# The 49-product in-projection for one more chunk: which chunk, which engine and which stage make its weight forms

## The chip, the cores and the metric

The kernel runs on one core of one Trainium2 chip. A core has five engines that run side by side: TensorE (PE, matmuls into PSUM), VectorE (DVE), ScalarE (ACT), GpSimd (POOL) and SyncE (SP, which issues DMAs). The metric is the device time of one execution in microseconds (us), lower is better; several executions are run and the median is given.

## The reference

Attention in which a query sees only the keys that fall to the same centroid, then a feed-forward block with the gate `h * erf(softplus(h))`. Batch 4, 8 heads, 768 positions, head size 64, all float32:

```python
q_assign = np.argmax(np.einsum('bhsd,hcd->bhsc', q_n, c_n), axis=-1)
k_assign = np.argmax(np.einsum('bhsd,hcd->bhsc', k_n, c_n), axis=-1)
mask = q_assign[:, :, :, None] == k_assign[:, :, None, :]
scores = np.where(mask, scale * np.matmul(q, k.transpose(0, 1, 3, 2)), -1000000000.0)
attn = softmax(scores)
x = np.matmul(attn, v).transpose(0, 2, 1, 3).reshape(3072, 512)
h = x @ w_in                                   # 512 -> 2048
sp = np.maximum(h, 0.0) + np.log1p(np.exp(-np.abs(h)))
out = (h * erf(sp)) @ w_out                    # 2048 -> 512
```

(`softmax` stands for the shifted exponentials and their division.) The change lies in the second part, `x @ w_in`, and in the work around it.

## The kernel before

**Attention** takes the first 408 us: 16 periods, one for each pair of heads of a batch. The transposed result x goes to a DRAM buffer, `x_dram`. Beside it the weights are converted and laid down in SBUF, and sums and differences of blocks of `w_in` ("left forms") are made, on DVE and on POOL. Ten conversion steps of `w_out` are left for later.

**The feed-forward part** takes the 3072 tokens in 6 chunks of 512. Each chunk has an in-projection (x times `w_in`), the gate (curves on ACT, products on DVE) and an out-projection. Products of 2x2 blocks are done with seven multiplications in place of eight (Strassen's scheme in Winograd's form), for which blocks are first added and subtracted; these sums are called *forms*. There are three ways of doing it:

- `hidden(n, lot)` does half an in-projection: 4 column groups of 7 products each, 28 products of two 128x128x256 matmuls. Each product goes to one of 8 PSUM banks in turn (`bank()`, six named `bank` and two named `turned`) and is then added into the output tile `g` by DVE or copied by ACT. `project(n, lot, pace)` does half an out-projection in the same way. While products are issued, other work is put between them, one item or more behind each product, from a list written by hand (`aside_work`).
- `hidden26` is `hidden` for chunks 1 and 2, and `project26` is an out-projection of 26 products, for chunks 1 to 5. Its right-hand forms are made once, on POOL, and streamed from DRAM (`b_dram`) through three SBUF places (`ring`).
- `hidden49(n)` does a whole in-projection with two levels of the scheme: 49 slots (`SLOTS`), each four 128x128x128 matmuls. It needs forms of the forms of `w_in`. With an outer form `o` (seven of them, the left forms of `w_in`), the inner ones are b12 - b11 (5), b22 - that (6), that - b21 (4) and b22 - b12 (7). Forms 4, 5 and 6 of each `o` lie in DRAM (`w_dram`, 21 blocks of 256 KB) and are streamed through `ring` (`load_twice`); form 7 takes the place of b12 in SBUF.

`TWICE = 3`: chunks 3, 4 and 5 use `hidden49`. Their forms are made by `forms_twice` on POOL: four of the 28 behind chunk 1's in-projection, the other 24 during chunk 2's, in a free x tile with four places; SP stores each to `w_dram`. `last_form_twice` then copies the seven forms 7 back from DRAM into `w_in`, when chunk 2's in-projection has read it for the last time.

**What orders the work.** Each engine runs its instructions in program order (`InOrder` wraps PE, DVE, ACT, POOL and one handle of SP, `sy`); DMAs issued by `nc.sync` itself may be put elsewhere in SP's queue. What matters around the change:

- The ten late conversion steps of `w_out`: each is a fetch by SP into one of four places, `size` and `rest` and `sign` on ACT, `bounded` and `shifted` on DVE, and `summed` on POOL, behind which the fetch of the step four later is issued. `weights(n)` lists them, `all_weights(lo, hi)` joins them.
- `out_forms[f]`: four POOL operations each, forms of `w_out`. `out_forms[0]` and `[1]` run in chunk 0's first in-projection half, `[2]` and `[3]` in chunk 1's first, behind a one-column POOL operation (`fence`) that waits for this half's first result.
- x tiles: `x_of[n]` are two buffers (`x_own`). `load_x(n)` reads a chunk's x from `x_dram`; `right_forms` of it are four operations.
- `a_s` (one buffer) holds the gate's curves.

All instructions carry line 132, that of the helper that records them, so the profile is read by the names of tiles. The order of stages is written out at the end of the kernel: chunk 0's in-projection halves, its first out-projection half, chunk 1's first in-projection half, chunk 0's second out-projection half, and then the loop over chunks.

Of the kernel before, what the change touches and what calls it, by code (L numbers as in the profile page):

```python
# [19 lines left out]
P = 128  # L20
# [94 lines left out]
WHERE = {"x": (0, 0), "u": (0, 1), "w": (1, 1)}  # L115
TWICE = 3
AHEAD = 4
BY_VECTOR = 4
GROUPS = (((1, 2), (1, 5, 6, 3, 7, 2, 4)), ((6, 7, 4), (1, 2, 5, 6, 3, 7, 4)), ((3, 5), (1, 5, 6, 3, 7, 2, 4)))
SLOTS = [(i, o) for inner, outer in GROUPS for o in outer for i in inner]  # L120
# [20 lines left out]
def kernel(  # L141
# [634 lines left out]
    def idle(n):  # L776
        return [lambda: None] * n
# [39 lines left out]

    ring, extra = [], []
    x_extra, spare_more = {}, []
    w_dram = dram.tile([len(STREAMED) + len(STEPS), P, FG * P], F32, name="w_dram")  # L820
    b_dram = dram.tile([N_STREAM + len(KEPT), P, FG * HM], F32, name="b_dram")
# [93 lines left out]

    def hidden26(n, lot, generation=(), later=()):
        generation = list(generation)
# [18 lines left out]
        else:  # L936
            aside_work.extend(paired([]))
        def begin():
            if later:
                fence(n)  # L940
            for work in later:
                work()

        hidden(n, lot, {0: begin, 1: middle})
        finish_aside()
# [23 lines left out]

    def forms_twice():  # L970
        t = xp.tile([P, DM // P, CT], F32, name="x_own").rearrange("p k t -> p (k t)")
        places = [t[:, i * FG * P : (i + 1) * FG * P] for i in range(4)]

        def made(o, i):
            w = lefts(*w_in_parts(0, HF))[o]
            b11, b12, b21, b22 = (w[:, k, f * FG * P : (f + 1) * FG * P] for k in range(2) for f in range(2))
            t, a, b = {
                5: (places[0], b12, b11), 6: (places[1], b22, places[0]),
                4: (places[2], places[1], b21), 7: (places[3], b22, b12),
            }[i]  # L980
            minus_of(t, a, b, ge)
            k = STREAMED.index((i, o)) if i < 7 else len(STREAMED) + STEPS.index(o)
            nc.sync.dma_start(out=w_dram[k], in_=t)

        return [functools.partial(made, o, i) for o in STEPS for i in (5, 6, 4, 7)]

    def last_form_twice():
        for o in STEPS:
            w = lefts(*w_in_parts(0, HF))[o]
            nc.sync.dma_start(out=w[:, 0, FG * P :], in_=w_dram[len(STREAMED) + STEPS.index(o)])  # L990

# [82 lines left out]
    def hidden49(n):  # L1074
# [3 lines left out]
        free = [banks[(k + i) % len(banks)] for i in range(len(banks))]  # L1078
        x_extra[n] = xp.tile([P, DM // P, CT], F32, name="x_own")
        x_forms, x_form = x_twice(n)  # L1080
# [125 lines left out]
    def project26(n):  # L1206
# [15 lines left out]
        else:  # L1222
            curves, products_at = gate_after(n)
        if n + 1 >= TWICE:
            load_x(n + 1)
        between = []
        if n + 1 < NCHUNK:
            parts = x_parts(n + 1)
            between = right_forms(ve, *parts)
            if n + 1 >= TWICE:  # L1230
                between = negated_last(between, ve, parts[2], parts[4])
        tiles = [(N_STREAM * (n - 1) + j + 2) % RING for j in range(N_STREAM)]
        banks26 = {}
# [35 lines left out]
        for p, r in enumerate(RIGHT):  # L1269
# [26 lines left out]
            if p >= len(RIGHT) - 4 and between:  # L1296
                between.pop(0)()
            if p == 12 and n + 2 < TWICE:
                load_x(n + 2)
        for p in sorted(banks26):  # L1300
# [188 lines left out]
    fetch(PLACES - 1)  # L1489
    queues[0] = queues[1] = nc.sync  # L1490
    for p in range(NPAIR):
        for i in range(HJ * 2):
            period(p, i)
        if p == LAST_X:
            load_x(0)
            load_x(1)
        if p == LAST_X + 2:
            forms += zip(*(right_forms(e, *x_parts(0)) for e in (ve, ge)))
# [28 lines left out]
    def weights(n):  # L1527
        return [
            functools.partial(w, N_EARLY + n) for w in (size_and_rest, bounded, sign, shifted, summed)
        ]  # L1530

    def all_weights(lo, hi):
# [3 lines left out]

    def fence(n=1):
        t = up.tile([P, HM], F32, name="u")
        g = g_of[n, 0, 0][:, 0, 0, 0:1]
        ge.tensor_tensor(out=t[:, 0:1], in0=g, in1=g, op=ALU.add)  # L1540
# [13 lines left out]
    finish_aside()  # L1554
    aside_work += gates(0, 0, (1,), right_forms(ve, *x_parts(1))) + gates(0, 1, (0,))
    project(0, 0, 3)
    finish_aside()
    aside_work += together(gates(0, 1, (1,)), idle(2) + [fence] + out_forms[2] + out_forms[3])
    take_places(2)
# [15 lines left out]
    for n in range(1, NCHUNK):  # L1575
        if n >= TWICE:
            hidden49(n)
        else:
            if n > 1:
                hidden26(n, 0, (), making if n + 1 == TWICE else ())  # L1580
            hidden26(n, 1, making if n == 1 else ())
        if n + 1 == TWICE:
            last_form_twice()
        if n + 2 == TWICE:
            making = forms_twice()
            for work in making[:AHEAD]:
                work()
            del making[:AHEAD]
        project26(n)
# [32 lines left out]
```

## Time and profile before

| | |
|---|---|
| median of 3 runs | 964.53 us (964.52 to 964.92) |
| profiled execution | 964.84 us, of which the profiled span is 963.1 us |
| TensorE | busy 954.6 us of the span |
| VectorE | busy 792.3 us |
| ScalarE | busy 535.9 us |
| GpSimd | busy 520.2 us |
| bytes read from and written to HBM | 86.54 MB and 26.21 MB |

TensorE's stages, by the start of the first matmul of each:

| starts at (us) | stage | length (us) |
|---|---|---|
| 407.95 | chunk 0 in-projection, two halves | 49.23 |
| 457.18 | chunk 0 out-projection, first half | 24.27 |
| 481.45 | chunk 1 in-projection, first half | 24.18 |
| 505.63 | chunk 0 out-projection, second half | 24.17 |
| 529.80 | chunk 1 in-projection, second half | 24.38 |
| 554.18 | chunk 1 out-projection | 44.95 |
| 599.13 | chunk 2 in-projection (`hidden26`, two halves) | 48.35 |
| 647.48 | chunk 2 out-projection | 44.89 |
| 692.37 | chunk 3 in-projection (`hidden49`) | 43.77 |
| 736.14 | chunk 3 out-projection | 45.19 |
| 781.33 | chunk 4 in-projection (`hidden49`) | 43.77 |

How to read the profile's rows: a row of an engine's instructions in order of time has the start (us from the start of the span), the duration (us) of the instruction or of a run of like ones, engine, line, operation, `out<-in` by the names of tiles with their shapes, the count, and in brackets the engine's idle time before it and what ended that. A float32 matmul shows as two records. PE's durations include the drain of its pipeline, so the distance between starts is the pace. In a row of windows each engine has its busy time and, in brackets, its instructions.

POOL by stage before: it is busy to 441.7 us nearly without a break, then works on single `summed` operations until 461.3, is idle to 484.2, busy from there to 560.5, idle to 601.6, busy to 634.

### The profile page before, as it was taken

What the parts mean: (1) busy time and instruction counts of PE and PEld (TensorE: products, weight loads), DVE (VectorE), ACT (ScalarE), POOL (GpSimd) and SP (SyncE); (2) the same over time, 40 slices, a digit from 0 to 9 for tenths busy, and PEclk for the clock granted to TensorE, in tenths of its full rate; (3) what the DMA queues carried; (4) which work ended last, traced back from release to release, by engine and by line L of the source; (5) the groups of instructions that cost most, each with busy time, mean ns of one, the idle gap of its engine ahead of it and who ended that gap; (6) DMA issues with size and microseconds to landing.
All of it is one profiled execution on the core that took longest, in us unless ns stands there. A gap on an engine that the chain in (4) does not pass through costs nothing.

```text
span 963.1 us, 22126 instructions
## 1 busy us (share of the span) xinstructions
PE 954.6 (99%) x8786; PEld 726.6 (75%) x8786; DVE 792.3 (82%) x1407; ACT 535.9 (56%) x806; POOL 520.2 (54%) x360
## 2 busy tenths in 40 slices
PE   8999999999999999999999999999999999999998
PEld 3555555555555555588888888888999899989987
DVE  8888888888888886879879888668868987896887
ACT  3777777777777665557614432354257236625541
POOL 1688888887788888845189920930054015202600
PEclk9999999999999999999999999999999999999999
DMA  9455444444444311051103454553445346344533
GB/s 211 87 111 111 111 111 110 108 109 106 89 111 111 67 35 35 19 182 45 44 1 153 154 197 138 222 198 104 160 123 173 110 132 208 110 144 122 159 113 110
DMA packets 171303, 114.20 MB, mean 119 GB/s; under 512 B 131264, under 2 KB 140992, under 8 KB 171200
## 3 DMA queue, kind: packets, MB, share of 16 engines
q1 hardware_dynamic: 168704, 112.36, 41.2%
q8 instruction: 69, 1.13, 0.5%
q10 hardware_dynamic: 2496, 0.43, 0.2%
q14 instruction: 34, 0.28, 0.1%
HBM read 86.54 MB, written 26.21 MB: 117 GB/s over the span
## 4 chain that ended last, share of the span: by engine, by line
PE 97%; DVE 1%; DMA 1%; SPq 0%; issue 0%; ACT 0%; DVEq 0%
PE bank L132 43%; PE turned L132 31%; PE sc L132 17%; PE wide L132 6%; DVE nmx L132 1%; DMA in_k<-in_k_dram 0%; SPq L132 0%; DMA in_q<-in_q_dram 0%; DVE kT L132 0%; DVE sims L132 0%; DVE qT L132 0%; DVE km L132 0%; DVE turned L132 0%; DVE wide L132 0%; ACT qm L132 0%
## 5 line engine op out<-in xcount | busy, mean ns | idle before, releaser
L132 POOL TENSOR_TENSOR more_out<-more_out,pr 128x768 f32<-128x768 f32 x128 | 217.3, 1697 | 18.5 <-ACT pr L132 9.9
L132 DVE TENSOR_REDUCE nmx<-wide 128x2 f32<-128x768 f32 x189 | 180.5, 955 | 47.9 <-PE wide L132 47.0
L132 ACT ACTIVATE pr<-sc 128x768 f32<-128x768 f32 x192 | 148.7, 810 | 94.0 <-PE wide L132 77.1
L132 PE MATMUL turned<-pr,in_v 128*32 128x193 f32 x3072 | 144.8, 330 | 0.0
L132 POOL TENSOR_TENSOR g<-g 128x512 f32<-128x512 f32 x27 | 35.4, 1310 | 178.8 <-DVE g L132 177.4
L132 PEld LDWEIGHTS turned<-pr,in_v 128*32 128x32 f32 x3072 | 91.5, 109 | 50.8 <-issue 21.3
L132 PE MATMUL sc<-qT,kT 64*128 64x384 f32 x528 | 98.3, 486 | 0.0
L132 DVE TENSOR_TENSOR g<-g 128x512 f32<-128x512 f32 x114 | 79.1, 694 | 19.8 <-PE bank L132 16.3
L132 DVE TENSOR_TENSOR g<-bank,g 128x256 f32<-128x256 f32 (+1 forms) x146 | 67.2, 476 | 27.3 <-PE bank L132 12.2
L132 PE MATMUL bank<-x_own,w_in 128*128 128x128 f32 (+1 forms) x464 | 83.8, 322 | 0.0
L132 DVE TENSOR_TENSOR g<-a_s,g 128x512 f32<-128x512 f32 x84 | 77.0, 938 | 3.6 <-ACT a_s L132 3.6
L132 PE MATMUL bank<-g_more,g 128*128 128x256 f32 x336 | 79.4, 379 | 0.0
L132 POOL TENSOR_TENSOR more_out<-pr,pr 128x768 f32<-128x768 f32 x32 | 60.4, 1886 | 28.1 <-ACT pr L132 28.1
L132 PEld LDWEIGHTS bank<-x_own,w_in 128*128 128x128 f32 x464 | 70.0, 191 | 6.0 <-issue 0.6
L132 PEld LDWEIGHTS bank<-g_more,g 128*128 128x128 f32 x336 | 63.8, 190 | 8.7
L132 ACT ACT_TABLE_LOAD x42 | 53.9, 1283 | 29.6 <-DVE g L132 29.0
L132 PE MATMUL bank<-w_out,g 128*128 128x256 f32 x296 | 69.3, 380 | 0.0
L132 ACT ACTIVATE a_s<-g 128x1024 f32<-128x1024 f32 (+1 forms) x38 | 42.7, 1143 | 45.5 <-POOL g L132 34.7
L132 PEld LDWEIGHTS <-qv 64*128 64x128 bf16 x384 | 27.0, 93 | 52.9 <-issue 36.7
L132 PEld LDWEIGHTS sc<-qT,kT 64*128 64x128 f32 x528 | 49.9, 187 | 21.4 <-ACT inv L132 2.4
L132 PE MATMUL wide<-kv,qv 64*128 64x384 bf16 x378 | 64.1, 328 | 1.3 <-DVE nmx L132 0.6
L132 PE MATMUL wide<-km,qm 64*128 64x384 bf16 (+1 forms) x378 | 62.6, 327 | 0.0
(236 smaller groups left out, 2004.9 us busy)
## 6 DMA issues: line engine op xcount, KB each, us to landing
g_more<-b_dram SPq DMA_DIRECT2D x48, 512.0 KB, 3.3
g_more<-w_dram SPq DMA_DIRECT2D x63, 256.0 KB, 2.9
w_dram<-x_own SPq DMA_DIRECT2D x28, 256.0 KB, 2.0
x_own<-in_moe_w_in_dram SPq DMA_DIRECT2D x13, 512.0 KB, 4.4
in_v<-in_v_dram SPq DMA_DIRECT2D x32, 192.0 KB, 3.1
x_dram<-more_out SPq DMA_DIRECT2D x128, 48.0 KB, 1.9
x_own<-x_dram SPq DMA_DIRECT2D x6, 1024.0 KB, 5.4
in_k<-in_k_dram SPq DMA_DIRECT2D x59, 96.0 KB, 2.8
```

The source lines that it names most:

```text
L132: ins = getattr(self.engine, name)(*args, **kw)
```

## The change

`TWICE` becomes 2: chunk 2 takes `hidden49` too, so only chunk 1 keeps the 28-product halves.

- The streamed forms 4, 5 and 6 of six of the seven outer forms (18 in all) are now made on POOL in chunk 0's in-projection: four right behind the attention (stored by `sy`), and 3, 3, 1, 1, 0, 1, 3, 2 of them ahead of the first eight `summed` (`MADE_BEFORE`, stored by `nc.sync`). Their places are the free `a_s` tile (four) and chunk 1's x tile `x_of[1]` (four, used again in turn).
- The three of the last outer form are made on POOL in chunk 1's out-projection, behind products 0, 2 and 4, and stored through ACT's queue two products later (`REST_AT`, `STORE_AFTER`).
- Form 7 is made in place by DVE, seven operations in chunk 1's out-projection behind products 3, 6, ..., 21 (`LAST_AT`); it no longer passes through DRAM, and `w_dram` has 21 blocks in place of 28.
- Since `x_of[1]` is used as a staging place, chunk 1's x is loaded behind chunk 0's in-projection, no longer in the attention, and its `right_forms` run in the second half of chunk 0's first out-projection instead of the first.
- `out_forms[2]` runs behind chunk 0's in-projection, ahead of that load.
- During the attention SP's loads keep their program order (`sy`).

```diff
-TWICE = 3
-AHEAD = 4
+TWICE = 2
+MADE_BEFORE = (3, 3, 1, 1, 0, 1, 3, 2, 0, 0)
+LAST_AT = (3, 6, 9, 12, 15, 18, 21)
+EARLY_OUTERS = 6
+STORE_AFTER = 2
+REST_AT = (0, 2, 4, 6, 8, 10, 12, 14, 16, 18, 20, 22)
...
-    def forms_twice():
-        t = xp.tile([P, DM // P, CT], F32, name="x_own").rearrange("p k t -> p (k t)")
-        places = [t[:, i * FG * P : (i + 1) * FG * P] for i in range(4)]
...
-        return [functools.partial(made, o, i) for o in STEPS for i in (5, 6, 4, 7)]
-
-    def last_form_twice():
-        for o in STEPS:
-            w = lefts(*w_in_parts(0, HF))[o]
-            nc.sync.dma_start(out=w[:, 0, FG * P :], in_=w_dram[len(STREAMED) + STEPS.index(o)])
+    def forms_twice(outers, staged):
+        places = [t[:, i * FG * P : (i + 1) * FG * P] for t in staged for i in range(4)]
+        n = 0
+        for o in outers:
+            w = lefts(*w_in_parts(0, HF))[o]
+            b11, b12, b21, b22 = (w[:, k, f * FG * P : (f + 1) * FG * P] for k in range(2) for f in range(2))
+            new = [places[n + i if n + i < len(places) else -4 + (n + i) % 4] for i in range(3)]
+            n += 3
+            for i, t, a, b in zip((5, 6, 4), new, (b12, b22, new[1]), (b11, new[0], b21)):
+                minus_of(t, a, b, ge)
+                yield functools.partial(store_queue[0].dma_start, out=w_dram[STREAMED.index((i, o))], in_=t)
+
+    def last_forms_twice():
+        work = {}
+        for o, p in zip(GROUPS[1][1], LAST_AT):
+            w = lefts(*w_in_parts(0, HF))[o]
+            b12, b22 = (w[:, k, FG * P :] for k in range(2))
+            work.setdefault(p, []).append(functools.partial(minus_of, b12, b22, b12, ve))
+        return work
...
+        making = {}
+        if n + 1 == TWICE:
+            x_extra[TWICE] = xp.tile([P, DM // P, CT], F32, name="x_own")
+            making = last_forms_twice()
+            store_queue[0] = ae
+            forms = forms_twice(GROUPS[1][1][EARLY_OUTERS:], [x_extra[TWICE].rearrange("p k t -> p (k t)")])
...
+            for p in REST_AT[: 3 * (len(STEPS) - EARLY_OUTERS)]:
+                making.setdefault(p, []).append(form)
+                making.setdefault(p + STORE_AFTER, []).append(store)
...
-            if p == 12 and n + 2 < TWICE:
-                load_x(n + 2)
+            for work in making.get(p, ()):
+                work()
...
-    queues[0] = queues[1] = nc.sync
+    queues[0] = queues[1] = sy
...
         if p == LAST_X:
             load_x(0)
-            load_x(1)
...
-            functools.partial(w, N_EARLY + n) for w in (size_and_rest, bounded, sign, shifted, summed)
+            functools.partial(w, N_EARLY + n) for w in (size_and_rest, bounded, sign, shifted, summed_after_forms)
         ]
+
+    making = forms_twice(
+        GROUPS[1][1][:EARLY_OUTERS],
+        (actp.tile([P, 2 * FG * HT], F32, name="a_s"), x_of[1].rearrange("p k t -> p (k t)")),
+    )
+    for _ in range(4):
+        next(making)()
+    queues[0] = store_queue[0] = nc.sync
+
+    def summed_after_forms(n):
+        for _ in range(MADE_BEFORE[n - N_EARLY]):
+            next(making, idle(1)[0])()
+        summed(n)
...
     finish_aside()
-    aside_work += gates(0, 0, (1,), right_forms(ve, *x_parts(1))) + gates(0, 1, (0,))
+    for store in making:
+        store()
+    for work in out_forms[2]:
+        work()
+    load_x(1)
+    aside_work += gates(0, 0, (1,)) + gates(0, 1, (0,), right_forms(ve, *x_parts(1)))
     project(0, 0, 3)
     finish_aside()
-    aside_work += together(gates(0, 1, (1,)), idle(2) + [fence] + out_forms[2] + out_forms[3])
+    aside_work += together(gates(0, 1, (1,)), idle(2) + [fence] + out_forms[3])
...
-            if n > 1:
-                hidden26(n, 0, (), making if n + 1 == TWICE else ())
-            hidden26(n, 1, making if n == 1 else ())
-        if n + 1 == TWICE:
-            last_form_twice()
-        if n + 2 == TWICE:
-            making = forms_twice()
-            for work in making[:AHEAD]:
-                work()
-            del making[:AHEAD]
+            hidden26(n, 1, making)
         project26(n)
```

## The prediction

> **What bounds the kernel now.** I read the page's busy times and its chain of waits first, then each engine's instructions in order of time from 400 us on. The page says that TensorE (PE) is the bound:
>
> ```profile
> span 963.1 us, 22126 instructions
> PE 954.6 (99%) x8786; PEld 726.6 (75%) x8786; DVE 792.3 (82%) x1407; ACT 535.9 (56%) x806; POOL 520.2 (54%) x360
> ...
> PE 97%; DVE 1%; DMA 1%; SPq 0%; issue 0%; ACT 0%; DVEq 0%
> ```
>
> 97% of the chain that ended last is matmul, so a saved matmul is saved time, and any other engine costs time only where it makes PE wait. The gain is read from the starts of PE's stages. These rows begin chunk 2's in-projection (old form), chunk 2's out-projection, chunk 3's in-projection (49 products), its out-projection, and chunk 4's in-projection:
>
> ```profile
> 599.13 1.03 PE L132 MATMUL turned<-x_own,w_in 128*128 128x256 f32 x4
> 647.48 1.89 PE L132 MATMUL turned<-more_out,g_more 128*128 128x256 f32 x8
> 692.37 1.95 PE L132 MATMUL bank<-x_own,w_in 128*128 128x128 f32 x16
> 736.14 1.89 PE L132 MATMUL bank<-more_out,g_more 128*128 128x256 f32 x8
> 781.33 1.84 PE L132 MATMUL bank<-x_own,w_in 128*128 128x128 f32 x15
> ```
>
> The old in-projection takes 647.48 - 599.13 = 48.35 us (56 products of 0.864), the new one 736.14 - 692.37 = 43.77 us (49 slots of 0.893).
>
> The other view is the end of chunk 0's second in-projection half, where PE has no slack left:
>
> ```profile
> 450.15 1.03 PE L132 MATMUL bank<-x_more,w_in 128*128 128x256 f32 x4
> 456.20 1.03 PE L132 MATMUL bank<-x_more,w_in 128*128 128x256 f32 x4
> 457.18 1.13 PE L132 MATMUL bank<-w_out,g 128*128 128x256 f32 x4
> ...
> 456.72 0.41 DVE L132 TENSOR_TENSOR g<-g,bank 128x256 f32<-128x256 f32 x1
> 445.00:457.00 12.00, 12.00 (x57) 10.43 (x55) 12.00 (x25) 6.94 (x9) 2.59 (x2) 1.00 0.13 44
> ```
>
> Products rotate over 8 PSUM banks. The product begun at 450.15 is the 21st of this half, and the first product of the out-projection, 8 later, reuses its bank. It starts at 457.18 and not at 456.20 + 0.864 = 457.06: it waits for DVE's eviction, which ends at 456.72 + 0.41 = 457.13. The windows row (columns PE, PEld, DVE, ACT, POOL) has DVE busy 12.00 of 12.00 us there. So DVE is one whole bank rotation behind, and **any delay of DVE before 456.72 is PE's delay in full**. Nothing wins it back, since PE is the chain afterwards.
>
> What can delay DVE there is POOL:
>
> ```profile
> 449.10 1.31 POOL L132 TENSOR_TENSOR w_out<-w_out,osb 128x512 int32<-128x512 int32 x1 [4.48 <-DVE w_out L132]
> 455.23 1.28 POOL L132 TENSOR_TENSOR w_out<-w_out,osb 128x512 int32<-128x512 int32 x1 [4.82 <-DVE w_out L132]
> 437.74 1.46 POOL L132 TENSOR_TENSOR w_out<-w_out 128x512 f32<-128x512 f32 x1
> 553.73 1.71 POOL L132 TENSOR_TENSOR x_own<-w_in 128x512 f32<-128x512 f32 x1
> ...
> 449.22 1.74 DVE L132 TENSOR_TENSOR g_more<-g 128x512 f32<-128x512 f32 x1
> 451.22 0.68 DVE L132 TENSOR_TENSOR g_more<-g_more,g 128x512 f32<-128x512 f32 x1
> ```
>
> A DVE addition on 128x512 with both inputs in SBUF takes 0.68 us while POOL idles (451.22). Begun just after POOL's (449.22 after 449.10), it ends 0.55 us after POOL's end. TENSOR_SCALAR does likewise: 0.41 us alone, else POOL's end + 0.28 (435.15 took 1.49). Operations that read PSUM stay at 0.41 beside a busy POOL. POOL pays as well: its pitch of 1.24 us (432.63, 433.86, 435.09) grows by 0.18 for a TENSOR_SCALAR let in (437.74) and by 0.45 for an addition (553.73 to 558.76, and pairs of 3.41 where quiet pairs take 2.50). One such DVE operation gets in per POOL operation. The Trainium skill (SBUF — State Buffer, "Who interferes with whom") calls this an exclusive lock on a port pair shared by VectorE and GpSimd: a VectorE instruction with two SBUF inputs, or in a two-port mode, fully blocks behind a GpSimd instruction. The rows agree, and this rule speaks against the change; without it the sum would be the bare -4.3 us.
>
> **The change part by part.** *Chunk 2's in-projection*: -(48.35 - 43.77) = -4.58 us. Its DVE, ACT, POOL and stream loads (20 more) are those of chunks 3 to 5, whose 49 slots ran without a gap on PE.
>
> *The out-projection behind it* lasts 647.48 to 692.37 = 44.89 now; the two that follow 49 products and precede others last 736.14 to 781.33 and 825.10 to 870.29, 45.19 each. +0.30 us.
>
> *Removed at no price*: 28 POOL forms and stores at 553.7 to 634, and 7 copies back through DRAM at 642 to 647. PE waited for none.
>
> *18 forms on POOL in chunk 0*: 4 behind the last attention sums (which end at 403.05 + 8.39 = 411.44), then 3, 3, 1, 1, 0, 1, 3, 2 ahead of summed 0 to 7. POOL's order up to the 18th form is 18 forms, 7 sums and 8 out-forms = 33 operations. A triple of forms takes 605.70 - 601.78 = 3.92 (one reads the result just made: pitch 1.35), so 6 x 3.92 = 23.5; 7 sums x 1.24 = 8.7; 8 out-forms, 2 of them at 1.35, 10.1. Together 42.3. In this time DVE wants in with 15 TENSOR_SCALARs (bounded and shifted 0 to 6, bounded 7) and 8 additions (an x form, four gate products, three left forms): 15 x 0.18 + 8 x 0.45 = 6.3. POOL ends at 411.44 + 48.6 = 460.0, without a pause, where it now idles 4.48 and 4.82 us.
>
> From 444 us on DVE then gets one SBUF operation per POOL operation, and its seventh bounded ends at 460.0 + 0.28. To the 21st eviction it has left (starts 0.33 apart, 0.60 for an addition): an eviction 0.33, an addition 0.60, two evictions 0.66, shifted 0.33, an eviction 0.33, bounded 8 behind POOL's next sum 1.2, the eviction 0.33 = 3.8. That is 464.1 against 457.13: +7.0. If the let-in operations fill the 12 gaps of 0.11 behind dependent forms (1.3), +5.7. I take +6.4, the middle. High end: the ninth form waits for the fifth's place to be stored; if that store stands in SP's queue behind the x_dram writes of 420.52, all comes 1 us later, +8.0. Low end: 33 x 1.24 = 40.9 with nothing paid for what is let in; POOL ends at 452.4, the eviction at 456.5, below today's, so 0.
>
> Earlier, in the first half, I find no PE wait: there the eviction most behind ends 3.2 us after its product (417.32 against 414.1), my delays add up to 1.9 by 424, and the limit is 7 x 0.864 = 6.05. By 433.5 DVE has caught up.
>
> *The sums behind the forms, and their fetches*: summed 4 slides from 440.40 to about 446, and the fetch behind it by 4 us; ACT's read of that place at 446.94 slips 3 us, but the DVE work that waits for it stands at 455.35 now and about 461 then. Nothing.
>
> *Chunk 1's x load and forms* move past SP's queue behind the forms' stores: the last store about 462, the load of 5.4 us (page, 1024 KB) lands at 468; DVE comes to these four additions at 471.5 + 6.4. They fall where DVE idled 2.94 us (before 475.74). If the load came 10 us later, DVE and so PE would stand behind it.
>
> *Four out-forms* (5.1 us) go from POOL at 484 to about 467, ahead of the gate products at 466.11, which ACT moves on with PE. At most 0.3 us late, where the first product that needs all four comes 1.7 us later. Nothing.
>
> *Chunk 1's out-projection*: seven in-place subtractions on DVE, 7 x 0.60 = 4.2 us, against 6.1 us of DVE idle there (1.98 before 563.02, 0.68, 0.36, 0.18, 1.63 before 588.97, 0.73, 0.58). Three forms on POOL instead of four. Three stores issued by ACT, each 4 us after its form by position, and ACT is busy 11.13 of 24.7 us in 559.0 to 583.7: evictions queue behind them, none late. Nothing; bounds 0 and what rival C gives.
>
> *SP's queue in attention* takes its loads in written order and the x load at 306.38 is gone. in_v is issued at 340.58 and the next at 364.92, each a period of 24.3 us ahead of use. Nothing; bound in rival D.
>
> **The sum**, against the profiled execution's own 964.84 us (span 963.1, 1.7 around it): 964.84 - 4.58 + 0.30 + 6.4 = 966.96. That execution lay 0.31 above the median of the runs, 964.53, so I say **966.7**. 0.2% of the time, 1.93 us, is about what a measurement of this kernel can tell from no change.
>
> **The rivals.** *A, the forecast*: the wait moves to PE at 452 to 464 us. With a delay of 4 to 8.3 us it gives 964.2 to 968.6; chance 0.66.
>
> *B, the other side*: DVE keeps its place, because POOL's pauses absorb the forms. For it: POOL is idle 9.3 us between 444.6 and 455.2. Against: 33 operations fill them. It decides from a delay under 2.3 us: 964.53 - 4.28 + 0 to 2.3 = 960.2 to 962.6; 0.25.
>
> *C, slower by chunk 1's out-projection*: the seven DVE subtractions wait as 449.22 does, 7 x 1.42 = 9.9 against 6.1 of idle, and carry 3.8 us into the 49 products. Banks there come free about 5 us ahead (evicted at 699.8, reused at 704.9), so it decides only with 1.2 us more, say behind ACT's stores. On top of A up to 3 us, 968 to 970; 0.05.
>
> *D, no gain arrives*: chunk 2's streamed forms, or a load in attention, come late. Against: 99% PE in chunks 3 to 5 and in attention. A plus 1 to 4.6; 0.04.
>
> **How the numbers follow.** A lies 0.41 above 966.46, 0.24 within, 0.01 below. B gives 0.23 faster and 0.02 same; C and D 0.07 slower, 0.02 same. Faster 0.24, same 0.28, slower 0.48. The range 961.8 to 968.6 leaves out the lower half of B (0.12) and C and D's upper part (0.07); A's own is 964.2 to 968.6.
>
> **What would show it.** Right: POOL without a pause from 411 to about 460; additions of DVE at 1.3 to 1.5 us there; PE gaps between 452 and 464 of some 6 us in all, and the first `bank<-w_out,g` of chunk 0 near 463.5; chunk 2's in-projection 43.8 us; nothing else on PE. Wrong: that first product still near 457 (then B), or PE gaps near 600 (C) or before 400 (D). In those gaps the Trainium skill (TensorE: Matmul & The Clock Gate, "What's actually happening") would halve the clock after an idle window of some 3.4 us; my longest gap is about 2.2 us, and the page's clock row is 9 throughout, so I add nothing for it.

## The result, and the profile after

The changed kernel takes **967.92 us** (median of 7 runs, 967.59 to 968.93); the kernel before, timed beside it, 964.89 us (7 runs). The ratio is 1.0035, 95% interval 1.0023 to 1.0046: slower by 0.35%. The prediction was 966.7 us. The profiled execution after takes 967.78 us, of which the span is 966.1 us, 3.0 more than before.

The same parts of the page as before, for the changed kernel (busy times by engine, then the chain of waits):

```profile
span 966.1 us, 22439 instructions
PE 953.0 (99%) x8954; PEld 729.1 (75%) x8954; DVE 810.8 (84%) x1399; ACT 540.8 (56%) x815; POOL 536.7 (56%) x370
...
PE 93%; DVE 3%; DMA 1%; ACT 1%; issue 1%; SPq 0%; DVEq 0%; ACTq 0%
```

PE is busy 1.6 us less (953.0 for 954.6), yet the span is longer: the saved matmuls are there, and so are new waits. In the chain PE's share falls from 97 to 93%, and DVE's rises from 1 to 3%. Where the waits stand is read from the starts of PE's stages, in the profiled executions:

| stage | before | after | difference |
|---|---|---|---|
| up to chunk 0's in-projection | 407.95 | 407.41 | -0.54 |
| chunk 0's in-projection | 49.23 | 56.54 | **+7.31** |
| chunk 0's and 1's next four halves | 97.00 | 96.80 | -0.20 |
| chunk 1's out-projection | 44.95 | 44.90 | -0.05 |
| chunk 2's in-projection | 48.35 | 43.77 | **-4.58** |
| chunk 2's out-projection | 44.89 | 45.19 | +0.30 |
| chunk 3's in-projection | 43.77 | 44.35 | +0.58 |
| all behind it | 226.96 | 227.14 | +0.18 |

The gain is exactly there. These are PE's instructions in order of time at the borders of chunk 2's in-projection, its first product and the first of its out-projection: 649.42 - 605.65 = 43.77 us.

```profile
605.65 0.61 PE L136 MATMUL turned<-x_own,w_in 128*128 128x128 f32 x4
649.42 1.89 PE L136 MATMUL turned<-more_out,g_more 128*128 128x256 f32 x8
```

The loss is at the end of chunk 0's in-projection. First PE, at the stage's start and there, with its idle time and what ended it in brackets, then POOL and DVE in the same stretch: 463.95 - 407.41 = 56.54 us.

```profile
407.41 1.99 PE L136 MATMUL bank<-x_own,w_in 128*128 128x256 f32 x8
...
453.27 1.13 PE L136 MATMUL bank<-x_own,w_in 128*128 128x256 f32 x4 [1.77 <-DVE g L136]
454.96 1.13 PE L136 MATMUL bank<-x_more,more_in 128*128 128x256 f32 x4 [0.56 <-DVE g L136]
456.65 1.13 PE L136 MATMUL bank<-x_own,w_in 128*128 128x256 f32 x4 [0.56 <-DVE g L136]
459.73 2.07 PE L136 MATMUL turned<-x_more,more_in 128*128 128x256 f32 x4 [1.95 <-DVE g L136]
461.60 1.66 PE L136 MATMUL turned<-x_own,more_in 128*128 128x256 f32 x4
463.09 1.03 PE L136 MATMUL bank<-x_more,w_in 128*128 128x256 f32 x4
463.95 2.32 PE L136 MATMUL bank<-w_out,g 128*128 128x256 f32 x10
...
457.47 1.59 POOL L136 TENSOR_TENSOR x_own<-x_own,w_in 128x512 f32<-128x512 f32 x1
461.41 1.28 POOL L136 TENSOR_TENSOR w_out<-w_out,osb 128x512 int32<-128x512 int32 x1 [2.35 <-DVE w_out L136]
...
453.14 1.43 DVE L136 TENSOR_TENSOR g_more<-g 128x512 f32<-128x512 f32 x1
456.52 1.42 DVE L136 TENSOR_TENSOR g<-g 128x512 f32<-128x512 f32 x1
459.60 0.67 DVE L136 TENSOR_TENSOR g_more<-g,g_more 128x512 f32<-128x512 f32 x1
462.90 0.41 DVE L136 TENSOR_TENSOR g<-g,bank 128x256 f32<-128x256 f32 x1
```

And the row of windows that had POOL busy 2.59 of 12 us before:

```profile
445.00:457.00 12.00, 9.11 (x41) 7.06 (x40) 12.00 (x15) 7.85 (x10) 11.92 (x8) 1.00 0.48 175
```

PE waits four times for DVE, for 4.84 us in all; the first of these waits ends at 453.27. DVE is busy without a break in either kernel, but does 15 instructions in these 12 us where it did 25: its additions with both inputs in SBUF take 1.42 to 1.44 us while POOL (now 11.92 us busy) makes forms, and 0.67 us at 459.60, half a microsecond after POOL's last form has ended (457.47 + 1.59 = 459.06). The eviction at 462.90, the one that releases the bank of the first out-projection product, ends 463.31, which is 55.90 us after the in-projection's start; before it was 457.13, or 49.18 after. So DVE is 6.72 us late.

Where this time goes can be added up. From DVE's last short pause (443.61 before, 443.70 after) to that eviction it does the same 26 operations in both kernels; the times are from each start to the next, in us:

| DVE's operations | before | after |
|---|---|---|
| 13 that read a PSUM bank | 4.34 | 4.31 |
| 8 additions and products with both inputs in SBUF | 6.39 | 9.26 |
| 5 TENSOR_SCALARs on `w_out` | 2.71 | 5.93 |
| together | 13.44 | 19.50 |

So 6.06 of the 6.72 us are longer SBUF operations of DVE in this stretch, and operations on PSUM take what they took. The other 0.6 us it brings along: its last pause of any size is 1.73 us for ACT before 440.88 (0.88 before 440.43 in the kernel before), and ACT had itself waited for DVE's `g` before its curve at 434.02. Neither of these waits ended with a transfer, and after 443.7 DVE does not wait at all.

PE is 7.31 late, 0.6 more. The rest is the clock. A row of windows per microsecond (the column behind the engines is the granted clock, the first of the last three):

```profile
459.00:460.00 1.00, 0.27 (x1) 0.27 (x2) 1.00 (x3) 0.00 (x0) 0.06 (x1) 0.72 0.08 31
460.00:461.00 1.00, 1.00 (x3) 0.82 (x4) 1.00 (x4) 0.00 (x0) 0.00 (x0) 0.50 0.59 231
461.00:462.00 1.00, 1.00 (x3) 0.76 (x3) 1.00 (x3) 0.00 (x0) 0.59 (x1) 0.50 0.00 0
462.00:463.00 1.00, 1.00 (x4) 0.80 (x3) 1.00 (x2) 0.00 (x0) 0.69 (x1) 0.57 0.75 61
```

From 459.45 to 462.86, by the trace's record of the clock, it is at half. The products begun at 459.73 and 461.60 take 1.87 and 1.49 us from start to start in place of 0.864. The last products before the out-projection then end late by themselves, and its first one starts 0.64 us after the eviction, where before it was 0.05.

### The profile page after: what moved, and what is told of

Its sections match the earlier page's. It is cut to its first block, busy times and chain, and to the rows that moved or that the text cites. A ratio compares the mean times of both kernels' runs of the same rounds, so it can differ in the third digit from the quotient of the medians.

```text
span 966.1 us, 22439 instructions
## 1 busy us (share of the span) xinstructions
PE 953.0 (99%) x8954; PEld 729.1 (75%) x8954; DVE 810.8 (84%) x1399; ACT 540.8 (56%) x815; POOL 536.7 (56%) x370
## 4 chain that ended last, share of the span: by engine, by line
PE 93%; DVE 3%; DMA 1%; ACT 1%; issue 1%; SPq 0%; DVEq 0%; ACTq 0%
PE bank L136 40%; PE turned L136 31%; PE sc L136 17%; PE wide L136 6%; DVE g L136 1%; DVE w_out L136 1%; DVE nmx L136 1%; DMA out_dram<-osb 0%; ACT a_s L136 0%; DMA in_k<-in_k_dram 0%; DVE osb L136 0%; SPq L136 0%; DMA in_q<-in_q_dram 0%; DVE kT L136 0%; ACT g_more L136 0%
## 5 line engine op out<-in xcount | busy, mean ns | idle before, releaser
L136 POOL TENSOR_TENSOR g<-g 128x512 f32<-128x512 f32 x36 | 47.1, 1309 | 217.5 <-DVE g L136 215.6
L136 PE MATMUL bank<-w_out,g 128*128 128x256 f32 x328 | 75.7, 380 | 0.0
L136 DVE TENSOR_TENSOR g<-bank,g 128x256 f32<-128x256 f32 (+1 forms) x129 | 63.7, 522 | 13.1 <-PE bank L136 5.9
L136 PE MATMUL bank<-x_own,w_in 128*128 128x128 f32 (+1 forms) x432 | 72.0, 309 | 2.3 <-DVE g L136 2.3
L136 PE MATMUL bank<-g_more,g 128*128 128x256 f32 x304 | 71.8, 379 | 0.0
L136 PEld LDWEIGHTS bank<-w_out,g 128*128 128x128 f32 x328 | 62.1, 190 | 9.6 <-issue 1.4
L136 PEld LDWEIGHTS bank<-x_own,w_in 128*128 128x128 f32 x432 | 60.9, 192 | 7.0 <-DVE g L136 3.1
L136 PEld LDWEIGHTS bank<-g_more,g 128*128 128x128 f32 x304 | 57.8, 190 | 7.8
```

What stands on the lines that cost most here:

```text
L136: ins = getattr(self.engine, name)(*args, **kw)
```

## The experiments

All medians and ratios are against the kernel before, run on the same chip beside it. "Early" forms are POOL's weight forms in chunk 0's in-projection; the changed kernel has 18 of them there and 3 in chunk 1's out-projection.

**1. Are POOL's forms the cause, or the DMAs that go with them?** The 18 subtractions are left out, and 18 stores copy a block of `w_in` in their place, so what chunks 2 to 5 compute is not the reference's result.

```diff
-                minus_of(t, a, b, ge)
+                if len(staged) == 1:
+                    minus_of(t, a, b, ge)
+                else:
+                    t = b11
                 yield functools.partial(store_queue[0].dma_start, out=w_dram[STREAMED.index((i, o))], in_=t)
```

> The 18 early subtractions on POOL are left out (chunks 2 to 5 read streamed forms that are only copies of a block of w_in), but all 18 stores, their places in SP's queue, the later load of chunk 1's x and the seven in-place subtractions of DVE stay. Port theory (DVE waits behind POOL's instructions): POOL is as free as before the change in 411 to 461 us, the first out-projection product of chunk 0 comes 49.2 to 49.6 us after the start of the in-projection, as before (49.23; with the change 56.54), and the time is 964.9 - 4.3 + 0 to 0.7 = 960.6 to 961.3. Rival, DMA theory (256 KB stores delay the fetches of the late weight steps, ACT reads them late, and that is what DVE and PE wait for): the 56.5 us and about 968 stay.

Measured: 960.38 us, ratio 0.9955 (0.994 to 0.9969). The in-projection takes 49.11 us, the other stages are as after within 0.3 us. The first products of this stage and of the next, and then the stores (duration, then first and last start):

```profile
407.87 1.99 PE L136 MATMUL bank<-x_own,w_in 128*128 128x256 f32 x8
456.98 3.19 PE L136 MATMUL bank<-w_out,g 128*128 128x256 f32 x14
...
L1559 SPq DMA_DIRECT2D w_dram<-more_in x9: 337/432/457, 344.2 to 369.4; - x9
L1559 SPq DMA_DIRECT2D w_dram<-w_in x5: 319/394/637, 74.1 to 371.0; - x5
L136 SPq DMA_DIRECT2D w_dram<-w_in x4: 439/536/917, 413.2 to 414.9; - x4
```

The edit took out more than it was meant to. A store of a block of `w_in` waits for no form, so 14 of the 18 left the stage with the forms: they are issued in the attention, by 371 us, and four at 413. The run shows that the whole +7.3 goes with the forms and their stores together, and that the later x load and the shifted out-forms cost nothing. Between forms and stores it does not decide; experiment 2 and DVE's times above do. It also gives the full worth of the 49 products: about -4.4 us.

**2. Is it what POOL reads, or that POOL is busy?** Each of the 18 subtractions becomes two memsets, which write the same place and read nothing; the streamed forms are then constants.

```diff
-                minus_of(t, a, b, ge)
+                if len(staged) == 1:
+                    minus_of(t, a, b, ge)
+                else:
+                    for _ in range(2):
+                        ge.memset(t, 0.5)
```

> Each of the 18 early subtractions on POOL is replaced by two writes of a constant into the same place (so the streamed forms of chunks 2 to 5 are constants): POOL is busy in the same places and reads nothing. If only POOL's reads hold up DVE's additions, as the port rule has it, the DVE additions of 444 to 460 us that fall beside a write last 0.7 us and not 1.4, TENSOR_SCALARs may still wait, and the first half of the delay goes: 51 to 54 us from the in-projection's start to the first out-projection product. If POOL's order alone (the sums behind the forms, the fetches behind the sums) sets the delay, it depends on POOL's time only: with writes as long as the subtractions (2 x 0.6 us) 56 us. If any POOL instruction blocks DVE, 55 to 57 us.

Measured: 961.92 us, 0.997 (0.9959 to 0.9981); in-projection 51.72 us in the profiled execution (962.9 us, the slowest of eight). Here all 18 stores are issued in the stage, from 413.2 to 456.6 us, as in the changed kernel, so they and what they push back cost 2.6 of the 7.4 us at the most. POOL, then DVE, in order of time:

```profile
449.44 3.48 POOL L136 MEMSET x_own<- 128x512 f32 x6
452.88 1.30 POOL L136 TENSOR_TENSOR w_out<-w_out,osb 128x512 int32<-128x512 int32 x1
...
449.97 0.85 DVE L136 TENSOR_SCALAR w_out<-w_out 128x512 uint32<-128x512 uint32 x1
451.07 0.68 DVE L136 TENSOR_TENSOR g_more<-g 128x512 f32<-128x512 f32 x1
452.00 0.68 DVE L136 TENSOR_TENSOR g_more<-g_more,g 128x512 f32<-128x512 f32 x1
452.94 1.79 DVE L136 TENSOR_TENSOR g<-g 128x512 f32<-128x512 f32 x1
```

Beside memsets an addition with two inputs in SBUF takes its 0.68 us; beside the next POOL operation that reads two (452.88) it takes 1.79. TENSOR_SCALAR (0.41 alone) waits even for a memset. In the stretch added up above, the 26 operations take 16.80 us (19.50 after, 13.44 before): the additions and products 7.34, near the 6.39 of before, the TENSOR_SCALARs 5.13, near the 5.93 of after. So most of the loss, not all of it, goes with POOL's reads, and what is left stands in DVE's operations again. The shares are not exact, since POOL is also done earlier, at 456.55 us in place of 459.06. The Trainium skill (SBUF — State Buffer, "Who interferes with whom") states both halves of this: a VectorE instruction with two SBUF inputs contends with a GpSimd instruction that reads SBUF and not with one that only writes it, while tensor_scalar in a two-port mode needs the shared pair itself. The four durations above agree with it.

**3. Fewer early forms.** Twelve early, nine in chunk 1's out-projection.

```diff
-MADE_BEFORE = (3, 3, 1, 1, 0, 1, 3, 2, 0, 0)
-EARLY_OUTERS = 6
+MADE_BEFORE = (3, 3, 1, 1, 0, 0, 0, 0, 0, 0)
+EARLY_OUTERS = 4
```

> Only 12 forms early (4, then 3, 3, 1, 1 ahead of the first four sums; none in the second in-projection half), the other 9 in chunk 1's out-projection. Port theory: out-forms still end at about 444.4 us, then POOL has only the sums; DVE meets two more busy POOL instructions than before the change: the in-projection lasts 49.2 + 1 to 2 us, and the time is 964.9 - 4.3 + 1 to 2 + 0 to 0.7 = 961.6 to 963.3, if nine forms on POOL in chunk 1's out-projection cost nothing (its 44.9 us stay). Rival: POOL's forms cost the same wherever they lie; then chunk 1's out-projection grows by 3 us or more and the time stays at 967 to 968.

Measured: 964.65 us, 1.0 (0.999 to 1.0009), outside what was expected. The in-projection takes 51.27 us as expected, but chunk 1's out-projection takes 47.66 in place of 44.90. PE in that stage:

```profile
572.45 1.99 PE L136 MATMUL turned<-g_more,g 128*128 128x256 f32 x8 [0.72 <-DVE g L136]
582.90 3.69 PE L136 MATMUL bank<-w_out,g 128*128 128x256 f32 x16 [1.54 <-DVE g L136]
```

**4. The forms where POOL and DVE both have room.** Nine early, in POOL's pauses; six right behind the in-projection, where DVE idles 3 us waiting for ACT's curves; six in chunk 1's out-projection. `out_forms[2]` goes back to its old place.

```diff
-MADE_BEFORE = (3, 3, 1, 1, 0, 1, 3, 2, 0, 0)
-EARLY_OUTERS = 6
+MADE_BEFORE = (1, 2, 1, 1, 0, 0, 0, 0, 0, 0)
+EARLY_OUTERS = 5
+FIRST_OUTERS = 3
...
-    for work in out_forms[2]:
-        work()
     load_x(1)
-    aside_work += gates(0, 0, (1,)) + gates(0, 1, (0,), right_forms(ve, *x_parts(1)))
+    middle = forms_twice(
+        GROUPS[1][1][FIRST_OUTERS:EARLY_OUTERS], (x_of[0].rearrange("p k t -> p (k t)"),)
+    )
+
+    def made():
+        next(middle)()
+
+    aside_work += gates(0, 0, (1,)) + together(
+        gates(0, 1, (0,), right_forms(ve, *x_parts(1))), [made] * (3 * (EARLY_OUTERS - FIRST_OUTERS))
+    )
     project(0, 0, 3)
     finish_aside()
-    aside_work += together(gates(0, 1, (1,)), idle(2) + [fence] + out_forms[3])
+    aside_work += together(gates(0, 1, (1,)), idle(2) + [fence] + out_forms[2] + out_forms[3])
```

> Nine forms early, laid into POOL's pauses (4, then 1, 2, 1, 1), six in chunk 0's first out-projection half, where POOL idled from 461 to 484 us, through the x tile that chunk 0 no longer needs, and six in chunk 1's out-projection; the second group of out-forms goes back to where it was. Port theory: POOL's out-forms end about 1.3 us later than before the change, the in-projection lasts 49.2 + 0 to 1 us; in the out-projection half a bank is reused after 8 x 1.73 us, so six blocked DVE additions (6 x 0.8 = 5 us) do not reach PE. Time 964.9 - 4.3 + 0 to 1 + 0 to 0.7 = 960.6 to 962.3, faster than both kernels. Rival: the wait only moves into the out-projection half, which grows by 2 to 5 us: 963 to 967.

Measured: 962.65 us, 0.998 (0.997 to 0.9989): faster than both kernels, and 0.35 us above the expected 960.6 to 962.3. The in-projection takes 49.11 us, the same as with no form at all, and the half behind it 24.22. What is left is in chunk 1's out-projection, 49.08 us in the profiled execution (the slowest of the ten). There PE waits once:

```profile
571.20 3.25 PE L137 MATMUL turned<-g_more,g 128*128 128x256 f32 x8 [2.13 <-DVE g L137]
```

Behind that wait the clock (0.50) falls in this execution, as the window of the next microsecond shows; the other nine have a mean clock of 0.999 or 1.000 where this one has 0.998.

```profile
572.00:573.00 1.00, 1.00 (x4) 0.74 (x4) 0.97 (x2) 0.00 (x0) 0.00 (x0) 0.50 0.00 0
```

**5. The last six held back** until product 12 of that stage, by a one-column POOL operation that reads an output tile.

In 4's kernel:

```diff
-REST_AT = (0, 2, 4, 6, 8, ...)
+REST_AT = (12, 13, 14, 15, 16, 17)
...
+            def hold():
+                t = up.tile([P, HM], F32, name="u")
+                o = osb_of[n, 0][:, 0, 0:1]
+                ge.tensor_tensor(out=t[:, 0:1], in0=o, in1=o, op=ALU.add)
+
+            making.setdefault(REST_AT[0], []).append(hold)
```

> The fourth experiment again, but the six last forms are held back on POOL until chunk 1's out-projection has come to its 12th product (a one-column POOL operation that reads an output block DVE has written by then), since the trace of the fourth showed PE waiting 2.13 us at its tenth product for a left step of DVE, which POOL's forms had pushed back, and the clock halved behind that. Theory (a POOL form costs only where the DVE work that it meets has no slack): chunk 1's out-projection 45 to 46 us in place of 49.1, the rest as in the fourth; 960.6 to 961.8. Rival (POOL's forms cost there wherever they lie): 47 to 49 us, 962 to 964.

Measured: 964.59 us, 0.9998 (0.999 to 1.0007), 1.9 us more than 4; the stage takes 48.80 us. My theory fell: the gap at 571 us goes, but four new ones come, of 0.43, 0.70, 0.39 and 0.68 us, each behind DVE. Two of them:

```profile
588.02 1.99 PE L137 MATMUL bank<-more_out,g 128*128 128x256 f32 x8 [0.70 <-DVE g L137]
595.10 1.99 PE L137 MATMUL bank<-g_more,g 128*128 128x256 f32 x8 [0.68 <-DVE g L137]
```

With the seven in-place subtractions in it, DVE has no idle time from 564 to 606 us, so the six forms cost there too.

**6. The order of SP's loads in attention** is put back in the changed kernel (`queues[0] = queues[1] = nc.sync`).

> The changed kernel with one part undone: SP's loads of the attention are free in their order again. The attention of the changed kernel was 0.54 us shorter than before in the profiled executions (407.41 against 407.95). If the pinned order did that: 407.9 to 408.0 here, and the time 0.5 above the changed kernel's 967.9. If it is chance or the x load that is gone: 407.4 to 407.9 and no more than 0.3 of difference.

Measured: 967.72 us, 1.0029 (1.0017 to 1.0041); 0.2 below the changed kernel, so the order does nothing that shows in the time. Attention ends at 408.09 us, as expected if the order shortens it. In the eleven kernels with the pinned order that end lies between 407.41 and 407.87, in the two without it at 407.95 and 408.09. So most of the table's -0.54 is no more than kernels with the same order differ by; whether the order brings a few tenths stays open. (The profiled execution, 969.5 us, is the slowest of six: its clock was at half for 6.83 us behind a PE gap of 1.97 us.)

**7. As 5, with `out_forms[2]` ahead of the six forms** behind the in-projection, as in the change.

> The fifth with the four operations of the second group of out-forms ahead of the six forms in chunk 0's first out-projection half, as in the change: POOL is then busy to about 473 us and not 468, beside the left forms of DVE (470.6 to 473.5), whose second PE awaited with 0.05 us to spare in the fourth. Port theory: four additions of DVE each 0.8 us later, PE waits 1.5 to 3.5 us there, that half lasts 25.7 to 27.7 and not 24.2. Rival (only the in-projection half is sensitive, the slower turn of banks covers all else): 24.2 to 24.4.

Measured: 968.58 us, 1.0038 (1.0024 to 1.0052). That half takes 29.05 us in place of 24.2, more than the 25.7 to 27.7 expected, with the clock at half for 3.41 us in it: ten POOL operations no longer fit where DVE idles, and the last forms meet the gate products and left forms.

```profile
475.73 3.57 PE L137 MATMUL bank<-more_out,g_more 128*128 128x256 f32 x8 [2.22 <-DVE g_more L137]
```

**8 and 9. Three, or all six, of the last forms at 496 us** instead, behind the out-forms of chunk 1's first in-projection half. In 4's kernel (9 has `EARLY_OUTERS = 7` and `[made] * 6` at the end):

```diff
-EARLY_OUTERS = 5
+EARLY_OUTERS = 6
...
-    aside_work += together(..., idle(2) + [fence] + out_forms[2] + out_forms[3])
+    aside_work += together(..., idle(2) + [fence] + out_forms[2] + out_forms[3] + [made] * 3)
```

> The kernel of e4_in_the_gap, with three of the six forms that it still makes in chunk 1's out-projection moved to 496 us, behind the out-forms of chunk 1's first in-projection half. The streamed forms of chunk 1's out-projection then end 3.9 us later on POOL (about 560.4 us instead of 556.5), and only three weight forms follow, without the pause for a store: POOL is done near 565.3 us instead of 570.0. Theory (what counts in chunk 1's out-projection is how many POOL instructions DVE's additions and in-place subtractions meet there, about 8 in either kernel, and the clock after a gap of 2 us): that stage falls from 49.08 to 46 to 48 us, at most a part of the 4.2 that it lost, and the time to 961.0 to 962.5. Rival 1 (only the weight forms behind 566 us cost, as in the changed kernel, where three of them cost nothing): stage 44.9 to 45.3 and 960.3 to 960.8. Rival 2 (the streamed forms come late for the products that use them): PE waits for a DMA into more_out or g_more in that stage, and 963 or more. The in-projection of chunk 0 stays at 49.1 and the half behind it at 24.2 in all.

> As e8_window with all six forms at 496 us, so that no weight form and no store through ACT's queue is left in chunk 1's out-projection; the streamed forms end on POOL near 564.3 us, 11 us into that stage. Theory: the same number of POOL instructions meets DVE there, 7 or 8; stage 46 to 48 us, time 961.0 to 962.5, within 0.6 of e8_window. Rival 1: the stage is back at 44.9 to 45.2, since no weight form is in it: 960.2 to 960.6. Rival 2 (late streams): PE waits for a DMA, 963 or more.

Measured: 968.9 us, 1.0045 (1.0032 to 1.0058), and 973.18 us, 1.0083 (1.0069 to 1.0097). Rival 2 holds: everything that POOL does behind 496 us slips, the streamed forms of chunk 1's out-projection with it, and PE has one wait there, for a transfer. In 8:

```profile
570.16 3.70 PE L137 MATMUL bank<-g_more,g 128*128 128x256 f32 x8 [6.03 <-DMA g_more<-b_dram]
```

POOL's last streamed form ended at 562.18 us, 8.0 before this product starts; in 4's kernel it ended at 556.5 and nobody waited. In 9 the wait is 9.59 us. A full POOL queue has deadlines behind it, and three forms put in ahead of them move them all.

**10. DVE's in-place subtractions out of the way.** In 4's kernel the first three move to behind products 13, 17 and 21, the other four to behind slots 12, 13, 17 and 18 of chunk 2's in-projection.

```diff
-LAST_AT = (3, 6, 9, 12, 15, 18, 21)
+LAST_AT = (13, 17, 21)
+LAST_SLOTS = (12, 13, 17, 18)
...
-            for f in also.get(at, ()):
+            for f in last_slots.get(n, {}).get(at, []) + list(also.get(at, ())):
```

> The kernel of e4_in_the_gap, with DVE's seven in-place subtractions moved: the first three from behind products 3, 6 and 9 of chunk 1's out-projection to behind 13, 17 and 21, the other four out of that stage, to behind slots 12, 13, 17 and 18 of chunk 2's in-projection, where DVE idles 1.17 us before 615.12 and 2.87 us before 618.68 in e4_in_the_gap's profile; the slots that use them begin at 624 us or later. Theory (in chunk 1's out-projection DVE has 6.1 us of idle time in all, of which the seven subtractions take 4.2 and POOL's forms at 556 to 570 us, by the waits that they force on DVE, the rest and more): up to 571 us DVE is relieved of a subtraction of 1.43 us beside POOL and of one of 0.60, together 2.0 us, against a PE gap of 2.13 us there, so the gap shrinks to 0.1 or vanishes, and the half clock behind it goes with it; the stage takes 44.9 to 45.6 us in place of 49.08, chunk 2's in-projection stays at 43.77, and the time is 959.9 to 960.9. Rival 1 (POOL's forms cost DVE and PE the same wherever the subtractions stand): stage 47 to 49 us, time 962 to 963. Rival 2 (the four subtractions delay evictions or the weight forms in chunk 2's in-projection): that stage takes 44.5 us or more.

Measured: 962.99 us, 0.9987 (0.9978 to 0.9996). By the medians this is no faster than 4 (962.65). Chunk 2's in-projection stays at 43.77 us, so four subtractions are free there. But chunk 1's out-projection takes 47.39 us: PE's gap shrinks from 2.13 to 1.59 us only, and my theory missed its size. DVE spent what it had gained waiting, 1.69 us for PE's product before 562.47 and 0.44 us for ACT's curves before 564.48; it falls behind only after that, beside POOL's last two forms.

**11. The last two POOL forms held to 584 us, all seven subtractions in chunk 2's in-projection.** In 10's kernel, with the `hold` of 5:

```diff
-LAST_AT = (13, 17, 21)
-LAST_SLOTS = (12, 13, 17, 18)
-REST_AT = (0, 2, 4, 6, 8, ...)
+LAST_AT = ()
+LAST_SLOTS = (7, 9, 12, 13, 17, 18, 20)
+REST_AT = (0, 2, 4, 6, 17, 19)
...
+            making.setdefault(REST_AT[4], []).append(hold)
```

> The kernel of e10_moved_on, with two edits. All seven in-place subtractions stand in chunk 2's in-projection now, behind slots 7, 9, 12, 13, 17, 18 and 20. And the last two weight forms of POOL, which ran at 567.6 and 569.4 us, are held back by a one-column operation that reads product 16's result, so that they run near 590 us, where DVE has the 1.8 us of the three subtractions that left. Theory (in e10_moved_on PE's 1.59 us before 571.57 come from POOL's two forms at 567.6 to 571, beside which two gate products took 2.36 us and the left steps followed late): that gap goes; at 590 the two forms cost DVE 2 times 0.75 against 1.8 us gained; what stays is the 0.40 us in which PE waited for a streamed form at 564.56. Stage 45.2 to 46.0 us in place of 47.39, and 960.6 to 961.6. Rival 1 (the forms cost the same wherever they lie in this stage, as in e5_held_back): stage 46.5 to 47.5, 962 to 963. Rival 2 (the subtractions delay chunk 2's in-projection, whose DVE is busy until 607 us): that stage takes 44.3 us or more.

Measured: **960.7 us**, 0.9958 (0.9944 to 0.9971), the fastest kernel here that makes all its forms, and 0.3 us above experiment 1, which leaves 18 of them out. The stage takes 45.24 us, chunk 2's in-projection 43.77. DVE's gate products and left steps, first in 10, then in 11:

```profile
567.49 2.36 DVE L138 TENSOR_TENSOR g<-a_s,g 128x512 f32<-128x512 f32 x2
569.77 3.92 DVE L138 TENSOR_TENSOR g<-g 128x512 f32<-128x512 f32 x4
```

```profile
567.43 1.28 DVE L138 TENSOR_TENSOR g<-a_s,g 128x512 f32<-128x512 f32 x2
568.64 2.86 DVE L138 TENSOR_TENSOR g<-g 128x512 f32<-128x512 f32 x4
...
584.10 3.24 DVE L138 TENSOR_TENSOR g<-g 128x512 f32<-128x512 f32 x2
```

The same six operations, begun at the same time, end at 573.69 beside POOL's two forms and at 571.50 without them: 2.2 us. At 584.10 the two forms cost DVE 1.8 us again (3.24 us for two additions that take 1.41 elsewhere), but PE does not wait there. Two things were changed at once, the place of the two forms and of the last three subtractions; the rows show what the forms did to DVE, and how much of the 2.3 us below experiment 10 each of the two brought stays open. (The hold let them go at 583.9 us, not at 590: the column that it reads was written earlier than product 16's result.)

## Why the prediction was right, and where its terms were off

*Chunk 2's in-projection, -4.58, and the out-projection behind it, +0.30*: exact, 43.77 and 45.19 us.

*DVE held behind POOL, +6.4*: the mechanism and the place are right, and the size lies within the 5.7 to 7.0 of which 6.4 was the middle. POOL has one pause, of 0.76 us, and its 18th form ends at 459.06 us; additions take 1.42 to 1.44 us; the eviction that counts is 6.72 us late against 6.4 said. The pause is the high end's condition: the ninth form does wait for a store, which stood in SP's queue behind the `x_dram` writes (419.99 us), for 0.76 us where I had put 1. DVE's times, added up, put all but 0.6 us of it into operations held beside POOL between 443.7 and 463.3 us, and the 0.6 comes by way of ACT from the first half, where the prediction had DVE caught up by 433.5. Nine early forms cost nothing, twelve 2.2 us and eighteen 7.4 us of that stage (49.11, 51.27, 56.54 against 49.11 without any; the clock's 0.6 is in the last). So, as placed in these kernels, there is slack first, and then each further form costs PE 0.7 to 0.9 us, about what one addition of DVE loses beside it (1.42 for 0.68). Rival B had the slack right, and the number of forms wrong.

*The clock, priced at nothing*: this is the term that failed. "My longest gap is about 2.2 us" held (1.95), but not "I add nothing for it": the clock went to half for 3.41 us, and that cost 0.6 us behind DVE's delay.

*Nothing for the sums and their fetches, the x load, the four out-forms, and SP's order in attention*: right as far as the runs show. ACT does wait for two of the late fetches, 1.71 us before 449.39 and 0.53 before 452.56, but DVE has no idle time there and its own times make up the delay, the half behind the in-projection takes 24.18 us, and undoing SP's order (experiment 6) leaves the time where it was. The four out-forms are free only there and then; experiment 7 charges 4.9 us, the half clock's share included, when six more forms follow them.

*Chunk 1's out-projection, nothing*: right for three forms and seven subtractions, 44.90 us. It was no large reserve: of 6.1 us of DVE idle time the subtractions take 4.2, and with six or nine forms the stage takes 47.7 to 49.1 us. The slack of 5 us in banks that I read for rival C doesn't help in that stage, since PE waits there for its operands, the left steps, which DVE makes just ahead of use.

*Chunk 3's in-projection*, +0.58, was in no term. ACT waits there 2.62 us for the output tiles of the stage before, whose stores land late, and PE behind it. It varies from kernel to kernel (this stage took 43.77 to 44.44 us in the profiles above, 43.77 in experiment 4), so it looks like a hazard of these stages rather than of a step of the change; no run here tests that.

Together, against the profiled execution's sum (966.96 said, 967.78 measured): +0.3 for DVE, +0.6 for the clock, +0.7 for late output tiles in chunks 3 and 4, -0.5 for attention's end, -0.3 in the halves and the stage that follow the in-projection. Between the medians (966.7 said, 967.92 measured) another 0.4 comes from the profiled executions, 0.31 above the median before and 0.14 below it after. That the smaller terms, +1.6 and -0.8 in all, cancel by half is luck.

## What to carry to other kernels

Price an operation that moves to an idle engine by what it does to the engine beside it: ask which instructions of the neighbour read SBUF twice in that stretch, how much slack the neighbour has there, and what else stands behind in the queue that now grows. The same POOL forms cost 7 us or 0.3, and the better places were found from one view, DVE's idle time by stage together with what ended it: a stretch in which DVE waits for ACT took six of them for 0.05 us; one in which its results are PE's next operands did not. And look where a run really put what an edit was meant to leave in place: experiment 1 kept its 18 stores in the program and lost 14 of them from the stage.

## What the runs showed of the hardware that was not expected

- **A little over 2 us of idle PE within one step of 3.41 us halves the clock for the next step.** In every trace here the recorded clock changes only after whole multiples of 3.413 us: in the changed kernel 133 such steps at full clock, one at half, 147 at full; two steps at half in experiments 6 and 8, three in 9. The grid starts at 5.3 to 7.9 us, differently in each execution. Cut by it, PE is idle for 2.13 us or more in the step before every fall (2.23 in the changed kernel, 2.13 in 4, 2.14 in 6, 2.28 in 7), and no step with 1.98 us or less is followed by one (1.98 at the end of 2, 1.88 in 9, 1.59 in 10, 1.54 in 3). So where a gap lies on the grid counts as well as its length. Two steps of the changed kernel, then one of experiment 10 (PE's busy time first, the clock third from the end):

```profile
456.03:459.45 3.42, 1.19 (x5) 0.68 (x4) 3.42 (x5) 0.00 (x0) 2.95 (x2) 1.00 0.20 77
459.45:462.86 3.41, 3.13 (x7) 2.52 (x8) 3.41 (x7) 0.00 (x0) 1.28 (x1) 0.50 0.40 92
...
569.48:572.90 3.42, 1.83 (x9) 1.30 (x8) 3.35 (x4) 0.00 (x0) 1.49 (x1) 1.00 0.03 10
```

The Trainium skill (TensorE: Matmul & The Clock Gate, "What's actually happening") puts the return to half clock after an idle window of some 3.4 us. The length of the steps agrees with it, but in these runs the step need not be idle throughout, and the measurement decides.
- **A POOL memset of 128x512 takes about 0.6 us** (six in 3.48 us, experiment 2) where a subtraction takes 1.3 to 1.8. Beside memsets DVE's additions take their 0.68 us, and a TENSOR_SCALAR is held for 0.44 us (0.85 for 0.41) where a subtraction holds it for up to 1.1 (1.49 for 0.41).
